# A gated mix of a long convolution and a two-row expert: forward transforms by four token residues and 256 frequencies, with VectorE additions behind them and a new table of order

## The chip, the cores and the metric

The kernel runs on one core of one Trainium2 chip. A core has five engines with a queue each: TensorE (PE in the profile, its weight loads PEld), VectorE (DVE), ScalarE (ACT), GpSimd (POOL) and SyncE (SP). Each engine takes its instructions in the order in which they stand in its queue; semaphores tie the queues together. TensorE writes to psum, eight banks of 512 float32 per partition; everything else lies in one large buffer of on-chip memory that the program calls RB. The metric is device time in microseconds, the median of the runs.

## The reference, cut to what matters

```python
# u: 2048 tokens x 512 channels (bf16), A, B, C: 512 x 128, complex
dt = exp(log_dt)[:, None]
P = exp((dt * A)[:, :, None] * arange(2048))           # all powers
K = einsum("dn,dnl,dn->dl", C, P, dt * B).real         # 512 kernels, 2048 long
y = irfft(rfft(pad(u)) * rfft(pad(K)))[:2048]          # a causal convolution per channel
a = y + u * Dskip
r = u @ w_r                                            # the two rows with the largest r
x2 = u[top2(r)]                                        # go through a gated MLP
b = u, with sigmoid(r) * ((silu(x2 @ w_gate) * (x2 @ w_up)) @ w_down) added to these two rows
g = sigmoid((u * gate_w).sum(-1))
out = g * a + (1 - g) * b
```

## The kernel before

The convolution is done with transforms that are matmuls with constant cosine and sine matrices. The 2048 tokens are two blocks m of 1024. Of each block the matmuls of the forward transform make 512 frequencies (four groups of 128, in two pairs kp), real and imaginary (the planes pl), for 512 channels. The tokens of a block stand as u(q, r): q is the half, r the residue of the token number modulo 4, with 128 tokens on the partitions.

`forward` (L716) makes one psum tile of two banks, 128 frequencies x 512 channels in each. For a plane and a pair kp, `product(par)` runs 8 matmuls of 128x512: two frequency groups, and four token groups (two halves, the two residues r = par and par + 2). First the odd residues (par 1) are accumulated, and `store` writes them scaled by -2 (fwo); then the even ones (par 0) are added into the same banks, and the sum is written (fwe). POOL then issues two accumulating transfers inside on-chip memory (ACC, L421, called vb), which add the second to the first: even tokens plus odd tokens, and even minus odd. That gives 1024 frequencies from 512. The frequency that lies 1024 higher needs no matmul of its own. The stores can be done by ScalarE (L403) or VectorE (L409, L733). Per block this is 64 matmuls (L723), eight stores of 1024 columns and four transfers of 256 KB.

The kernels K are built from powers: ScalarE makes exponentials of the decays (ep, eq; `AF`, L412) and sines of phases (sin), TensorE the phases (pa, L605, L606, L625, L627) in fixed point, VectorE multiplies them (`coarse`: pi, pr; `fine`: px, py, ps; all by `TT`, L387). `lags` multiplies coarse and fine powers on TensorE (kmm, L900, L901), evacuates them (kae), selects (sel, L914; kcx, kce), and `spectrum` turns them into spectra KH (ks, L941; khe). `products` multiplies spectra (prod, yr, yi, pq, b0, b2, b13 on VectorE; ac on TensorE with the stores ace), and `inverse` transforms back (iv, L1082 to L1087) with the stores ive (L1098, L1102) and the output transfers.

Beside it runs the routing: a transposed load of u (xt, L424, issued by SyncE), log (L660) with its copies rs, rf, the two largest rows (gm, gm2, L678 to L681), the gather gu, and the MLP (ff, dn, with transfers of its three weight matrices). Other names in the prediction: al and bs are the first VectorE instructions, on the loaded A; arg (L586) are phase arguments; dth is exp(log_dt) on ScalarE and dtn its cast on VectorE (L406); np (L400) are eight products of B and C with dtn; nw transposes their sums on TensorE, kw stores them; k0e, k0c store a row for lag 0; ns negates sines (L632).

What sets the order: the program adds its operations in one list; each names what it reads and writes and the engines that may do it. PLAN holds for every place in the order the number of an operation and which of its engines does it; BANKS holds a psum bank for each tile. `replay` (L111) walks PLAN and `emit_plan` (L135) puts each operation into its engine's queue with the waits that its data need. So a change of PLAN moves work between engines and in every queue. On chip memory is cut into regions by hand: F holds the forward matrix, later the constants of the spectra (kn); U holds u, then the second block's transform and small constants; V the transforms.

The lines where the accumulating transfer and the forward matmuls stand:

```python
def ACC(name, vs, rd, wr, kb):
    return P.add(name, [(POOL, 1.5 * len(vs), lambda h: [h.dma_start(out=o(), in_=a_(), accum_op=ALU.add) for o, a_ in vs])], ...)
...
for i, (q, r) in enumerate((q, r) for q in range(2) for r in (par, par + 2)):
    x = h.matmul(P32(t, k2, ...), FM(0, 128, pl * 4096 + (par * 4 + i) * 512 + (2 * kp + k2) * 128, (1, 128)), U(..., ((m * 2 + q) * 4 + r) * 512, (1, 512)), ...)
```

## Time and profile before

| | us |
|---|---|
| three runs | 152.25, 152.31, 152.98 |
| median | 152.31 |
| the profiled execution | 152.89 |
| its span, first to last instruction | 151.0 |

| engine | busy, us | instructions |
|---|---|---|
| TensorE | 139.5 | 1603 |
| VectorE | 135.5 | 186 |
| ScalarE | 116.5 | 173 |
| POOL | 27.6 | 34 |

The span is some 2 us shorter than the execution that it was taken from; the rest lies around the first and the last instruction. "Busy" counts an engine that executes; an idle engine is charged to whatever released it. A row of a view with "x60 | 71.6, 1221 | 0.7" says: 60 instructions, 71.6 us busy in all, 1221 ns for one, 0.7 us of idle time before them. A row of the view in order of time begins with its start and its length. Instructions of one engine can overlap at their ends, so the busy time of a group is a little less than count times mean.

### The profile page before, as it was taken

The numbers are of one execution on the slowest core, as the hardware profiler recorded it, in microseconds if no ns is written. First come the engines' busy times: TensorE is split into PE (matmuls) and PEld (weight loads), VectorE is DVE, ScalarE is ACT, GpSimd is POOL, SyncE is SP. The second block draws the span as 40 slices with busy tenths as digits, with TensorE's granted clock in tenths as the row PEclk, the third lists the DMA queues.
The fourth block names the chain that finished last, engine by engine and source line by source line (L and its number), as shares of the span: only waits on it lengthen the run. The fifth ranks groups of instructions, "written<-read, shape, count | busy, mean of one in ns | idle before, by whom it ended". The sixth has DMA issues, their size and how long they took to land.

```text
span 151.0 us, 3726 instructions
## 1 busy us (share of the span) xinstructions
PE 139.5 (92%) x1603; PEld 100.5 (67%) x1603; DVE 135.5 (90%) x186; ACT 116.5 (77%) x173; POOL 27.6 (18%) x34
## 2 busy tenths in 40 slices
PE   3799999999999999999875999999999999999990
PEld 2257776444664665898845889856878767776870
DVE  0699899999999999999999999999999999994941
ACT  4697998999999897667972778877994773379830
POOL 5000001300010199679206200220000000000000
PEclk9999999999999999999999999999999999999999
DMA  3899899980893096799971500018930009400176
GB/s 77 238 270 286 293 411 413 407 329 13 289 358 121 0 538 295 197 288 195 190 114 13 96 0 4 4 23 270 276 148 4 0 0 253 166 4 0 35 208 174
DMA packets 23107, 26.43 MB, mean 175 GB/s; under 512 B 9486, under 2 KB 20244, under 8 KB 22420
## 3 DMA queue, kind: packets, MB, share of 16 engines
q1 hardware_dynamic: 20644, 23.98, 49.3%
q0 software_dynamic: 2304, 2.10, 9.1%
q8 instruction: 12, 0.20, 0.5%
q10 hardware_dynamic: 144, 0.13, 0.4%
q14 instruction: 3, 0.02, 0.0%
HBM read 19.78 MB, written 4.20 MB: 159 GB/s over the span
## 4 chain that ended last, share of the span: by engine, by line
PE 55%; DVE 36%; issue 4%; DMA 1%; ACT 1%; SPq 0%; DVEq 0%
DVE RB L387 33%; PE psm L723 18%; PE psm L1087 7%; PE psm L1004 4%; PE psm L625 4%; PE psm L491 4%; PE psm L627 2%; PE psm L605 2%; PE psm L786 2%; PE psm L1082 2%; PE psm L1006 2%; PE psm L1008 2%; PE psm L660 1%; PE psm L531 1%; PE psm L606 1%
## 5 line engine op out<-in xcount | busy, mean ns | idle before, releaser
L387 DVE TENSOR_TENSOR RB<-RB 128x2048 bf16<-128x2048 bf16 (+6 forms) x113 | 106.8, 994 | 3.4 <-ACT RB L403 2.5
L403 ACT ACTIVATE RB<-psm 128x1024 bf16<-128x1024 f32 (+6 forms) x52 | 46.9, 944 | 13.0 <-PE psm L1008 7.3
L723 PE MATMUL psm<-RB 128*128 128x512 bf16 x128 | 29.1, 379 | 0.0
L412 ACT ACTIVATE RB<-RB 128x512 bf16<-128x512 f32 (+6 forms) x48 | 27.1, 646 | 1.7 <-DVE RB L387 1.6
L412 ACT ACTIVATE RB<-psm 128x1024 bf16<-128x1024 int16 (+2 forms) x23 | 21.6, 976 | 6.1 <-PE psm L627 4.4
L723 PEld LDWEIGHTS psm<-RB 128*128 128x128 bf16 x128 | 12.3, 98 | 13.2
L1087 PE MATMUL psm<-RB 128*128 128x256 bf16 x128 | 18.9, 273 | 0.0
L900 PE MATMUL psm<-RB 128*128 128x80 bf16 x256 | 17.5, 198 | 0.0
L901 PE MATMUL psm<-RB 128*128 128x64 bf16 x256 | 17.5, 191 | 0.0
L900 PEld LDWEIGHTS psm<-RB 128*128 128x128 bf16 x256 | 17.0, 96 | 0.6 <-DVE RB L387 0.2
L901 PEld LDWEIGHTS psm<-RB 128*128 128x128 bf16 x256 | 16.9, 97 | 0.1
L941 PE MATMUL psm<-RB 128*128 128x256 bf16 x128 | 14.3, 273 | 2.0 <-ACT RB L403 2.0
L941 PEld LDWEIGHTS psm<-RB 128*128 128x128 bf16 x128 | 12.4, 98 | 4.1 <-ACT RB L403 2.7
L1087 PEld LDWEIGHTS psm<-RB 128*128 128x128 bf16 x128 | 12.5, 98 | 1.6
L1098 ACT ACTIVATE RB<-psm,RB 128x256 bf16<-128x256 f32 x25 | 9.9, 478 | 3.1 <-PE psm L1087 3.1
L421 POOL DMA_DIRECT2D RB<-RB x8 | 9.9, 2188 | 2.4 <-ACT RB L403 2.4
L1004 PE MATMUL psm<-RB 128*128 128x512 bf16 x32 | 10.2, 379 | 0.2 <-DVE RB L387 0.2
L625 PE MATMUL psm<-RB 128*128 128x256 f16 x64 | 9.0, 273 | 0.5 <-ACT RB L412 0.5
L397 POOL CAST RB<-RB 128x16 bf16<-128x16 f32 (+4 forms) x6 | 6.9, 1165 | 12.9 <-DVE RB L670 12.8
L1082 PE MATMUL psm<-RB 128*128 128x256 bf16 x32 | 8.7, 273 | 0.0
L409 DVE CAST RB<-psm 128x1024 bf16<-128x1024 f32 (+3 forms) x7 | 7.2, 1025 | 0.9 <-PE psm L555 0.7
L625 PEld LDWEIGHTS psm<-RB 128*128 128x128 f16 x64 | 6.1, 98 | 2.2 <-ACT RB L412 0.8
(77 smaller groups left out, 161.3 us busy)
## 6 DMA issues: line engine op xcount, KB each, us to landing
RB<-c_fwd SPq DMA_DIRECT2D x2, 1024.0 KB, 8.0
RB<-in_A_u_dram SPq DMA_DIRECT2D x2, 1024.0 KB, 6.8
RB<-c_near SPq DMA_DIRECT2D x2, 1024.0 KB, 5.4
RB<-RB POOLq DMA_DIRECT2D x8, 256.0 KB, 9.0
RB<-u_routed SPq DMA_DIRECT2D x2, 1024.0 KB, 5.4
RB<-in_B_w_gate_dram SPq DMA_DIRECT2D x1, 1792.0 KB, 14.1
RB<-in_B_w_up_dram SPq DMA_DIRECT2D x1, 1792.0 KB, 14.3
RB<-in_B_w_down_dram SPq DMA_DIRECT2D x1, 1792.0 KB, 8.6
```

The source lines that it names most:

```text
L387: return P.add(name, [(eng, c_dve(n, mode) if eng == DVE else 1.6, lambda h: h.tensor_tensor(out=o(), in0=a_(), in1=b_(), op=op))], rd, wr ...
L403: return lambda h: h.activation(out=o(), in_=a_(), func=ACTF.Copy, scale=scale() if callable(scale) else scale)
L412: return P.add(name, [(ACT, cost or c_act(n), lambda h: h.activation(out=o(), in_=a_(), func=func, scale=scale))], rd, wr, table=table, **kw)
L421: return P.add(name, [(POOL, 1.5 * len(vs), lambda h: [h.dma_start(out=o(), in_=a_(), accum_op=ALU.add) for o, a_ in vs])], rd, wr, dma=(4 ...
L625: r = h.matmul(o, DGM(0, 128, d * 128, (1, 128)), HL(0, 128, z * 512 + hf * CW, (1, CW)), start=(u == 0 and z == 0 and i % 2 == 0), stop=F ...
L723: x = h.matmul(P32(t, k2, 0, 128, 0, (1, 512)), FM(0, 128, pl * 4096 + (par * 4 + i) * 512 + (2 * kp + k2) * 128, (1, 128)), U(0, 128, ((m ...
L900: h.matmul(P32(t, q // 6, 0, 128, (q % 6) * 80, (1, 80)), tp, TQv(0, 128, c * 10240 + ri * NT2 * 256 + r * 4, (256, NT2), (1, 4)), start=( ...
L901: x = h.matmul(P32(t, q // 6, 0, 128, (q % 6) * 80 + 16, (1, 64)), tp, ARENA(0, 128, eY[c][ri][0] + r * 4, (eY[c][ri][1] - eY[c][ri][0], 2 ...
L941: x = h.matmul(o, KN(0, 128, g * 2048 + col, (1, 128)), KC[c](0, 128, g * 256, (1, 256)), start=(g == 0), stop=(g == NG - 1))
L1004: r = h.matmul(P32(t, kt, 0, 128, 0, (1, 512)), CI(0, 128, 0, (1, 128)), f(k, 0, 512), start=(k == 0 and hc == 1), stop=False, skip_group_ ...
L1082: h.matmul(o, RD(0, 128, (tb + 8) % 16 * 128, (1, 128)), UE[q](0, 128, r * 256, (1, 256)) if early else U2(0, 128, tb * D + c * CW, (1, 25 ...
L1087: x = h.matmul(o, G(0, 128, (pl * 2 + kt // 2) * 1024 + (r * 2 + q) * 128, (1, 128)), PQ(0, 128, r * 1024 + kt * 256 + pl * 256 if quarter ...
```

## The change

The forward transform now makes one psum tile for each pair of residues. It computes only 256 frequencies (every other group of 128), but keeps the four residues apart: the two banks of a tile hold two residues instead of two frequency groups, and each takes 2 matmuls (the two halves) instead of 4. With z = 1 the tile holds residues 2 and 3, with z = 0 residues 0 and 1 added to them; the stores are scaled as before, and vb adds in the same way as before, now even and odd residues apart. A second step follows for each block: vs adds and subtracts the odd sums to the even sums, vt does the same with the quarter-turned differences (real and imaginary planes exchanged). That gives the same 1024 frequencies. Per block this is 32 matmuls instead of 64, the same eight stores and four transfers, and four VectorE instructions (`TT`) of 2048 elements per partition.

The forward matrix is half as large (two loads of 512 KB instead of 1024) and its region F lies elsewhere; its freed half holds some of the transform (fodd), which the first load of kn overwrites later. PLAN and BANKS are new throughout.

```diff
-PLAN = [(0, 0), (4, 0), (21, 0), (3, 0), (1, 0), (41, 0), (22, 0), (42, 0), (174, 0), ...
+PLAN = [(4, 0), (5, 0), (6, 0), (0, 0), (21, 0), (3, 0), (1, 0), (41, 0), (22, 0), (42, 0), (234, 0), ...
...
-    a = [np.outer(BLK + token(0, q, r), theta()) for par in range(2) for q in range(2) for r in (par, par + 2)]
+    th = theta().reshape(4, 128)[::2].reshape(256)
+    a = [np.outer(BLK + token(0, q, r), th) for r in range(4) for q in range(2)]
...
         def forward(m, pl, kp, behind):
             t = P.pst(2, "fw", (0, 2))
-            def product(par):
+            def product(z):
                 def fw(h):
                     x = None
                     for k2 in range(2):
-                        for i, (q, r) in enumerate((q, r) for q in range(2) for r in (par, par + 2)):
-                            x = h.matmul(P32(t, k2, 0, 128, 0, (1, 512)), FM(0, 128, pl * 4096 + (par * 4 + i) * 512 + (2 * kp + k2) * 128, (1, 128)), U(0, 128, ((m * 2 + q) * 4 + r) * 512, (1, 512)),
-                                         start=(par == 1 and i == 0), stop=(par == 0 and i == 3), skip_group_check=True)
+                        r = 2 * z + k2
+                        for q in range(2):
+                            x = h.matmul(P32(t, k2, 0, 128, 0, (1, 512)), FM(0, 128, pl * 2048 + ((r * 2 + q) * 2 + kp) * 128, (1, 128)), U(0, 128, ((m * 2 + q) * 4 + r) * 512, (1, 512)),
+                                         start=(z == 1 and q == 0), stop=(z == 0 and q == 1), skip_group_check=True)
                     return x
...
         def transform(m, behind=()):
...
-                ACC("vb", [(v(1, z), v(0, z)) for z in range(2)], [bV[m][0][pl], bVO[m][pl]], [bV[m][1][pl]], 512)
+                ACC("vb", [(vat(m, 1, 1024 - 512 * pl, (1, 512)), vat(m, 0, 1024 + 512 * pl, (1, 512))), (fodd(m, 512 * pl, (1, 512)), vat(m, 1, 1536 * pl, (1, 512)))], bFE(m, 0, pl) + bFE(m, 1, pl) + bOD(m, pl) + [bFO[m][pl]], bFE(m, 1, pl) + [bFO[m][pl]], 512)
+            e0, e1, od = [b[0] + b[1] for b in ([bFE(m, 0, pl) for pl in range(2)], [bFE(m, 1, pl) for pl in range(2)], [bOD(m, pl) for pl in range(2)])]
+            even, odd = vat(m, 0, 1024, (512, 2), (1, 512)), vat(m, 1, 0, (1536, 2), (1, 512))
+            TT("vs", vat(m, 0, 0, (512, 2), (1, 512)), even, odd, ALU.add, e0 + od, bV[m][0][0], 2048)
+            TT("vs", even, even, odd, ALU.subtract, e0 + od, e0, 2048)
+            quad, turn = vat(m, 1, 1024, (-512, 2), (1, 512)), fodd(m, 512, (-512, 2), (1, 512))
+            TT("vt", odd, quad, turn, ALU.add, e1 + bFO[m], od, 2048)
+            TT("vt", quad, quad, turn, ALU.subtract, e1 + bFO[m], e1, 2048)
```

The new table also gives some work of VectorE to ScalarE: one fwo store, one fwe store, three ns, k0e, a kcx, a kae, a k0c and two ive stores; one ace store goes the other way. ScalarE loads its function tables four times instead of five.

How the queues changed, at the places that the prediction speaks of. All names in these rows are RB and psm, so the lines tell the operations; the new file's lines lie 2 higher than those of before up to the transform, and up to 14 higher behind it.

SyncE, the first transfers. Before (in_A_B and in_A_C are the four inputs of np, in_A_u with DMA_TRANSPOSE is xt):

```order
L478 DMA RB<-in_A_log_dt_dram 1x512
L479 DMA RB<-c_id 128x128
L481 DMA RB<-in_A_A_im_dram 128x512
L498 DMA RB<-c_diag 128x896
L517 DMA RB<-in_A_Dskip_dram 1x512
L524 DMA RB<-in_A_log_dt_dram 128x4
L481 DMA RB<-in_A_B_re_dram 128x512
L481 DMA RB<-in_A_C_re_dram 128x512
L498 DMA RB<-c_diag 128x512
L481 DMA RB<-in_A_B_im_dram 128x512
L481 DMA RB<-in_A_C_im_dram 128x512
L424 DMA_TRANSPOSE RB<-in_A_u_dram 128x4x2048
```

and now:

```order
L480 DMA RB<-in_A_log_dt_dram 1x512
L481 DMA RB<-c_id 128x128
L483 DMA RB<-in_A_A_im_dram 128x512
L500 DMA RB<-c_diag 128x896
L526 DMA RB<-in_A_log_dt_dram 128x4
L426 DMA_TRANSPOSE RB<-in_A_u_dram 128x4x2048
L483 DMA RB<-in_A_C_re_dram 128x512
L483 DMA RB<-in_A_B_im_dram 128x512
L483 DMA RB<-in_A_B_re_dram 128x512
L483 DMA RB<-in_A_C_im_dram 128x512
L500 DMA RB<-c_diag 128x512
L520 DMA RB<-c_f 128x160
```

The transposing load moved ahead of the four inputs of np and of one part of c_diag; Dskip moved behind.

VectorE and ScalarE, the first instructions. VectorE now (L588 is arg, the CAST of 128x4 at L408 is dtn, the COPY from psm is log, L402 of 128x256 is np):

```order
L588 TENSOR_SCALAR RB<-RB 128x512
L389 TENSOR_TENSOR RB<-RB 128x512
L588 TENSOR_SCALAR RB<-RB 128x512 x7
L408 CAST RB<-RB 128x4
L588 TENSOR_SCALAR RB<-RB 128x512
L408 COPY RB<-psm 128x32
L588 TENSOR_SCALAR RB<-RB 128x512
L408 CAST RB<-RB 128x16 x2
L680 TENSOR_REDUCE RB<-RB 128x1
L402 SCALAR_TENSOR_TENSOR RB<-RB 128x256 x6
```

ScalarE now, between its first activation and its second table load (128x128x4 are ep, 128x2x256 and 128x512 are eq, 128x4 is dth):

```order
L414 ACTIVATE RB<-RB 128x128x4 x3
L414 ACTIVATE RB<-RB 128x2x256
L414 ACTIVATE RB<-RB 128x128x4
L414 ACTIVATE RB<-RB 128x2x256 x3
L414 ACTIVATE RB<-RB 128x128x4 x2
L414 ACTIVATE RB<-RB 128x2x256 x3
L414 ACTIVATE RB<-RB 128x128x4
L414 ACTIVATE RB<-RB 128x2x256
L414 ACTIVATE RB<-RB 128x128x4 x2
L414 ACTIVATE RB<-RB 128x4
L414 ACTIVATE RB<-RB 128x128x4
L414 ACTIVATE RB<-RB 128x512
```

Before, seven large activations stood ahead of dth, and VectorE had four arg ahead of dtn, the eight np mixed with further arg behind it, and log only after kw and the first weights. Now 17 stand ahead of dth, eight arg ahead of dtn, and log stands ahead of all np.

VectorE in the middle, the second half of the coarse powers with the new instructions. Now (128x2x64x16 are pi and pr, L634 is ns, 128x2x1024 and 128x2x2x512 are vs and vt):

```order
L389 TENSOR_TENSOR RB<-RB 128x2x64x16
L389 TENSOR_TENSOR RB<-RB 128x2x1024
L389 TENSOR_TENSOR RB<-RB 128x2x64x16
L389 TENSOR_TENSOR RB<-RB 128x2x1024
L634 TENSOR_SCALAR RB<-RB 128x1024
L389 TENSOR_TENSOR RB<-RB 128x2x64x16 x2
L389 TENSOR_TENSOR RB<-RB 128x2x2x512
L389 TENSOR_TENSOR RB<-RB 128x2x64x16
L389 TENSOR_TENSOR RB<-RB 128x2x1024
L389 TENSOR_TENSOR RB<-RB 128x2x64x16 x2
L389 TENSOR_TENSOR RB<-RB 128x2x2x512
L389 TENSOR_TENSOR RB<-RB 128x2x64x16
```

The two first rows of 128x2x1024 are vs of block 0; vt and the ones of block 1 follow between the coarse factors, all before the second half of the fine powers. Before, pi and pr stood there with ns, the px and py of the fine powers and one kae store between them.

46 lines of the change are left out of this document (25 added, 21 removed), and 67 rows, old and new, of the table PLAN.

## The prediction

> **What bounds the kernel now.** I read the page first (busy time of each engine, then the chain that ended last), then the busy time by stretch, then VectorE's waits, then the rows by shape.
>
> ```profile
> PE 139.5 (92%) x1603; PEld 100.5 (67%) x1603; DVE 135.5 (90%) x186; ACT 116.5 (77%) x173; POOL 27.6 (18%) x34
> PE 55%; DVE 36%; issue 4%; DMA 1%; ACT 1%; SPq 0%; DVEq 0%
> DVE RB L387 33%; PE psm L723 18%; PE psm L1087 7%; PE psm L1004 4%; PE psm L625 4%; PE psm L491 4%; PE psm L627 2%; PE psm L605 2%; PE psm L786 2%; PE psm L1082 2%; PE psm L1006 2%; PE psm L1008 2%; PE psm L660 1%; PE psm L531 1%; PE psm L606 1%
> ```
>
> The chain seems to convict TensorE: 55% of the span, and the forward matmuls of L723 alone 18%. These are what the change halves. But a chain shows one engine that was busy, not that the others had time to spare. The stretches show that. I cut at 4.25 us (VectorE's first instruction), at 62.7 (where the chain passes from TensorE to VectorE) and at 134.8 (the end of the last two products).
>
> ```profile
> 4.25:62.70 58.45, 57.42 (x517) 34.79 (x517) 55.66 (x95) 54.05 (x77) 12.64 (x17) 1.00 0.83 277
> 62.70:134.80 72.10, 68.22 (x984) 55.47 (x981) 71.49 (x77) 51.54 (x78) 12.82 (x12) 1.00 0.47 115
> 134.80:151.00 16.20, 12.13 (x103) 9.38 (x100) 8.33 (x15) 9.07 (x18) 0.00 (x0) 1.00 0.33 97
> ...
> DVE RB L387 <- PE psm L531: 4.3, 1, 4.3
> DVE RB L387 <- ACT RB L403: 2.5, 3, 2.0
> DVE RB L1102 <- PE psm L1087: 2.0, 3, 1.1
> DVE RB L409 <- PE psm L555: 0.7, 1, 0.7
> DVE RB L400 <- PE psm L531: 0.7, 1, 0.7
> DVE RB L400 <- issue: 0.2, 1, 0.2
> DVE RB L733 <- PE psm L723: 0.2, 1, 0.2
> ```
>
> Behind the length of a stretch stand the busy times of TensorE, its weight loads, VectorE, ScalarE and POOL. VectorE is busy 55.66 of 58.45 us, then 71.49 of 72.10. From its first instruction to 134.8 it does nothing for 3.4 us in all. So in the first stretch both engines are full, and TensorE's relief is worth to VectorE only what VectorE waits for TensorE there: 0.7 (L400), 0.7 (L409), 0.2 (L733). The wait of 4.3 is the start, behind the first loads; those of 2.5 and 2.0 lie in the last 16.2 us. VectorE's own work between 4.25 and 134.8 therefore sets the end, with some 16 us of tail behind it.
>
> **The work that VectorE gains and loses.**
>
> ```profile
> L387 DVE TENSOR_TENSOR RB<-RB 128x2048 bf16<-128x2048 bf16 x60 | 71.6, 1221 | 0.7
> L733 DVE TENSOR_SCALAR RB<-psm 128x1024 bf16<-128x1024 f32 x4 | 4.8, 1212 | 0.2 <-PE psm L723 0.2
> L409 DVE CAST RB<-psm 128x1024 bf16<-128x1024 f32 x3 | 3.7, 1222 | 0.8 <-PE psm L555 0.7
> L632 DVE TENSOR_SCALAR RB<-RB 128x1024 bf16<-128x1024 bf16 x7 | 2.9, 411 | 0.0
> L409 DVE CAST RB<-psm 32x512 bf16<-32x512 f32 x2 | 1.4, 696 | 0.1
> L409 DVE CAST RB<-psm 128x960 bf16<-128x960 f32 x1 | 1.2, 1158 | 0.0
> L919 DVE COPY RB<-RB 32x256 bf16<-32x256 bf16 x1 | 0.2, 223 | 0.0
> L403 ACT ACTIVATE RB<-psm 128x1024 bf16<-128x1024 f32 x36 | 35.3, 1021 | 9.3 <-PE psm L1008 7.3 <-PE psm L941 1.7 <-PE psm L946 0.3
> L723 PE MATMUL psm<-RB 128*128 128x512 bf16 x128 | 29.1, 379 | 0.0
> ```
>
> Added: eight tensor-tensor instructions of 128x2048 bf16 (vs twice and vt twice, for two blocks). Shape and type are those of the first row, and all inner runs are 512 long. 71.6 us over 60 is 1.19 each, so 9.5 us. Where such an instruction does not wait for the one before it, they follow each other closer, and in dependent pairs a little wider; I give the sum 0.5 us either way.
>
> Taken off VectorE and put on ScalarE by the new table: one fwo store (1.21), one fwe store (1.22; the row's third is kw and stays), three negations ns (3 x 0.41 = 1.23), k0e and kcx (2 x 0.70), a kae (1.16) and a k0c (0.22). That is 6.4. Net before the last products: +3.1 us. ScalarE does the big ones in about 1.0 us (its row), at 54.05 of 58.45 busy in the first stretch and 51.54 of 72.10 in the second; the moves come late in the first stretch or in the second, where there is room, and it saves a table load.
>
> TensorE loses 64 of 128 matmuls at 29.1/128 = 0.23 us, 14.5 us. All of it lies beside VectorE's work, so I cost it at nothing. If VectorE were not the cover, it would be worth 14.5.
>
> **The front, where the order is new.** Here a step is moved past queues. SyncE now issues the transposing load of u ahead of the four loads of B and C; ScalarE runs 17 exponentials before dth instead of seven large activations; VectorE has dtn and log ahead of the products np.
>
> ```profile
> 8.63 1.43 DVE L586 TENSOR_SCALAR RB<-RB 128x512 int32<-128x512 f32 x4
> 9.97 0.17 DVE L406 CAST RB<-RB 128x4 f32<-128x4 bf16 x1
> ...
> 4.97 5.41 ACT L412 ACTIVATE RB<-RB 128x512 bf16<-128x512 f32 x11 [1.63 <-DVE RB L387]
> 27.41 4.37 ACT L412 ACTIVATE RB<-RB 128x512 bf16<-128x512 f32 x9
> ...
> 2.49 0.29 SPq L517 DMA_DIRECT2D RB<-in_A_Dskip_dram  x1
> 3.22 0.43 SPq L481 DMA_DIRECT2D RB<-in_A_B_re_dram  x1
> 5.61 8.14 SPq L424 DMA_TRANSPOSE RB<-in_A_u_dram  x1
> RB<-in_A_u_dram SPq DMA_TRANSPOSE x1, 10.1
> RB<-in_A_C_im_dram SPq DMA_DIRECT2D x1, 128.0 KB, 3.2
> ...
> 18.11 2.26 PE L660 MATMUL psm<-RB 128*128 128x2 bf16 x64
> ```
>
> First dtn. ScalarE's exponentials start behind al at 4.97. Eleven there, one of them the tiny dth, take 5.41: 0.52 for a large one (the second row, eight large and one tiny in 4.37, says the same). Seventeen end at 4.97 + 8.8 = 13.8, dth at 14.0. VectorE comes to dtn after eight arg instructions (1.34 us for four, from 8.63 to 9.97): 8.63 + 2.7 = 11.3. It waits 2.7 us.
>
> Then log. The transposing load was issued at 5.61; the loads of B and C, one of c_diag and that of Dskip (0.34 from its start to the next) no longer stand ahead, so it starts at 3.22 - 0.34 = 2.9, lands 10.1 later at 13.0, and TensorE's 64 small matmuls take 2.26: log can be read at 15.3. VectorE is there at 14.0 + 0.17 + 0.42 = 14.6: another 0.7. Queued behind are arg, rs, gm and np, thus all of VectorE. np does not wait again: its four loads are issued from 2.9 + 8.1 = 11.0 on, about 0.48 apart (five in 3.22 to 5.61), the last near 12.5, and land 3.2 later at 15.7; np comes at about 16.4. The two waits are 3.4 us. Two old ones go: kw's 0.7, since its weights are now ready behind other work, and the 0.2 called issue. Net +2.5.
>
> **The accumulating transfers.** vs overwrites what vb reads, and vt needs its sums, so VectorE now waits in order for POOL's transfers; before, only the products far behind did.
>
> ```profile
> L421 POOL DMA_DIRECT2D RB<-RB x8: 1209/1929/3651, 59.7 to 69.0; - x8
> DMA to landing us min/median/max: 6.9/9.0/11.1
> ```
>
> For the first block I estimate the last store some 3 us behind VectorE's last fwo (seven large ScalarE instructions and a table load follow an sge that waits for ffe, against 5 us of VectorE from ffe to fwo); the second issue and the landing add 1.2 + 9.0 (at most 11.1): 13 to 15. From that fwo VectorE has eleven large and eight small instructions to do before the vs that waits, 11 x 1.2 + 2.4 = 15.6 us: hidden, narrowly. For the second block the last fwe follows a coarse sine that waits for a pr of VectorE, 1.9 us behind it; with 1.2 + 9.0 that is 12.1, and VectorE does ten large ones and a negation (12.4 us) between. Even, so I take 0; with the slowest landing it costs 1.8, which goes into the upper bound. The queued victims would be vs, vt and the second coarse factors, then kmm and the spectra.
>
> **The tail.**
>
> ```profile
> 138.83 0.38 PE L1087 MATMUL psm<-RB 128*128 128x256 bf16 x2
> 146.11 0.82 PE L1087 MATMUL psm<-RB 128*128 128x256 bf16 x6
> L1102 DVE TENSOR_TENSOR RB<-psm,RB 128x512 bf16<-128x512 f32 x3 | 2.1, 692 | 2.0 <-PE psm L1087 2.0
> L1102 DVE TENSOR_TENSOR RB<-psm,RB 128x256 bf16<-128x256 f32 x1 | 0.4, 421 | 0.0
> ```
>
> An ace store comes to VectorE (1.22) and two ive go from it (0.69 + 0.42). VectorE may lose 1 us of its wait for ScalarE there, but from 138.8 to the end of the row at 146.11 TensorE runs the inverse matmuls nearly without a gap, and their number and order behind the last products are as before. 16.2 us stay: 0, at best -0.5.
>
> **Sum.** 151.0 + 3.1 + 2.5 = 156.6 us of span. The profiled execution took 152.89, 1.9 more than its span, and lies 0.6 above the median 152.31. So 156.6 + 1.9 - 0.6 = 157.9; I say 157.8.
>
> **Rivals.**
>
> A, the sum above: 157.8; of its own 155.8 to 159.6.
>
> B, the work comes but not the front wait: the exponentials or the load are earlier than I work out, or the planner's order leaves VectorE something to do. 151.0 + 3.1 - 0.9 = 153.2 of span, 154.5. For it: the load now has less traffic ahead. Against it: dth and log bind independently, and each alone costs over 2 us.
>
> C, TensorE at half rate at log, so that the routing and everything behind is later still.
>
> ```profile
> 6.39 3.17 PE L491 MATMUL psm<-RB 128*128 128x512 bf16 x7 [0.78 <-DVE RB L400]
> 15.07 1.02 PE L491 MATMUL psm<-RB 128*128 128x512 bf16 x4
> ```
>
> Seven warm-up matmuls of one shape take 3.17 us early (0.45 each), four take 1.02 later (0.22 to 0.25), while the granted clock reads 1.00 throughout. Of the 16 warm-up matmuls in front, two now stand before the first use, two more before the forward transforms; the rest are moved to the middle. TensorE has nothing between about 5.6 and 9 us. If the 64 matmuls of log pay double, 2.3 us: 160.1. If they are bound by issue, nothing. The Trainium skill, "TensorE: Matmul & The Clock Gate", Part 1, says that the array runs at half its clock until some 3.4 us of sustained work, and falls back after an idle window as long. By that rule the pair of rows above is the rise, and C is likelier than not to cost part of its price; the granted clock in this trace does not show it.
>
> D, not slower: the chain is right, TensorE's 14.5 us come off the first 62.7, and the new additions fill holes. 151.0 - 14.5 + 9.5 = 146.0, or 147.3 by the median. For it: TensorE is busy 57.42 of 58.45. It decides only if VectorE's instructions, or their order, leave it 14.5 us to give; its idle time before 62.7 is 2.8. That is what speaks against it.
>
> **Chances.** A 0.60, B 0.18, C 0.14, D 0.05, and 0.03 for the sums of small gains that end near no change. Half a per cent is about what a measurement of this kernel can tell from none. Faster by more than that: D with a little, 0.06; within: 0.03; slower: 0.91. The range takes A and C whole and B's centre: 154.2 to 160.8 (C with a part of the 1.8 of the transfers).
>
> **What would show it.** VectorE's busy time near 138.6 and TensorE's near 125. A first VectorE wait of 2 to 3 us at the small cast dtn, released by ScalarE, and a shorter one at the copy of log, released by TensorE. The forward matmuls gone from the chain, VectorE's share above half. vs and vt at 1.2 us, with less than 2 us of waits for transfers. The last products ending near 140. It is wrong if VectorE is found idle for less than 3 us up to there (B), if its work did not grow by about 3, or if the tail shrank by more than 1.

## The result, and the profile after

| | before | after |
|---|---|---|
| runs, us | 152.25, 152.3, 152.31, 152.98 | 166.37, 166.71, 167.26, 167.92 |
| median | 152.31 | 166.99 |
| the profiled execution, and its span | 152.89, 151.0 | 166.71, 164.9 |
| granted clock over the span | 1.0 | 0.935 |

The ratio is 1.096, with an interval of 1.090 to 1.102. The prediction said 157.8, with a range to 160.8: the direction was right, the size was not. Of some variants below, single runs were granted a lower clock and took up to 5 us longer; the times given for these variants, like the ratios, leave such runs out.

First the page: busy time, the granted clock, and the chain.

```profile
PE 133.6 (81%) x1532; PEld 96.5 (59%) x1539; DVE 136.8 (83%) x184; ACT 122.7 (74%) x183; POOL 30.9 (19%) x34
PEclk9999569965699999999999699999999999999998
DVE 39%; PE 27%; DMA 16%; ACT 13%; issue 2%; POOL 0%; SPq 0%; DVEq 0%
DVE RB L389 31%; DMA RB<-RB 10%; PE psm L1101 7%; ACT RB L405 7%; ACT RB L414 5%; DMA RB<-in_A_u_dram,RB 5%; PE psm L1018 4%; DVE RB L402 3%; PE psm L607 2%; PE psm L1022 2%; PE psm L1020 2%; DVE RB L411 2%; PE psm L608 2%; PE psm L1096 2%; PE psm L662 1%
```

The forward matmuls (L729) have left the head of the chain, as the change means them to. But VectorE's share is 39%, not above half, and two kinds of transfer stand in a chain that had 1% of them: those inside on-chip memory (10%) and the gather (5%). VectorE's busy time hardly rose (135.5 to 136.8). So the 14 us are not work. The busy time by stretch, cut at VectorE's first instruction, around its longest idle time, and at the end of the last two products:

```profile
4.27:75.03 70.76, 52.86 (x585) 34.62 (x588) 61.82 (x100) 64.29 (x90) 25.96 (x26) 0.88 0.84 236
75.03:81.89 6.86, 6.83 (x143) 5.47 (x139) 0.00 (x0) 6.43 (x8) 0.00 (x0) 1.00 0.61 146
81.89:148.60 66.71, 58.95 (x703) 45.75 (x706) 66.47 (x70) 40.96 (x66) 2.82 (x1) 0.97 0.26 85
148.60:164.90 16.30, 12.17 (x103) 9.48 (x101) 8.53 (x15) 9.19 (x20) 0.00 (x0) 0.97 0.34 98
```

The third number with a count in brackets is VectorE's. It is busy 61.82 of 70.76 us, then for 6.86 us not at all, then 66.47 of 66.71. The tail is 16.30 us (16.20 before). Up to the last products VectorE works 61.82 + 66.47 = 128.29 us; before, the two stretches gave 55.66 + 71.49 = 127.15. Idle it is for 16.0 us, against 3.4. The whole difference of the spans, 13.9, is therefore +1.1 of work, +12.6 of waits and +0.1 of tail. VectorE's waits (total, times, longest) name them:

```profile
DVE RB L389 <- DMA RB<-RB: 6.9, 1, 6.9
DVE RB L408 <- ACT RB L414: 3.4, 1, 3.4
DVE RB L411 <- PE psm L729: 1.7, 1, 1.7
DVE RB L408 <- PE psm L662: 1.4, 1, 1.4
DVE RB L408 <- PE psm L707: 1.4, 1, 1.4
DVE RB L411 <- PE psm L557: 0.5, 1, 0.5
```

The first is the second vs of block 1, waiting for its accumulating transfers: 6.9 us, of which the prediction had 0, at most 1.8. L408 behind ScalarE is dtn, and L408 behind L662 is log: 3.4 and 1.4 (predicted 2.7 and 0.7). L408 behind L707 is xs, which waits for the gathered rows, and L411 behind L729 is the fwe store queued behind it on TensorE: 3.0 us together (1.37 and 1.66), and in no term of the sum. Behind 82 us there is no wait of this size until the tail.

Now the two unforeseen ones in order of time (start, length, engine). First the transfers of block 1 on POOL's queue, SyncE's issues, and the vs that ends the wait:

```profile
61.76 2.41 POOL L423 DMA_DIRECT2D RB<-RB  x2 [2.18 <-ACT RB L405]
63.90 0.34 SPq L1138 DMA_DIRECT2D RB<-c_near  x1
64.28 2.02 SPq L1140 DMA_DIRECT2D RB<-in_A_u_dram  x4
65.43 2.40 POOL L423 DMA_DIRECT2D RB<-RB  x2 [0.87 <-ACT RB L405]
66.34 0.86 SPq L832 DMA_DIRECT2D u_routed<-in_A_u_dram  x1
67.24 0.60 SPq L1139 DMA_DIRECT2D RB<-c_far  x1
81.89 15.09 DVE L389 TENSOR_TENSOR RB<-RB 128x2048 bf16<-128x2048 bf16 x13 [6.86 <-DMA RB<-RB]
```

The last two transfers are issued from 65.43 on, and vs can run at 81.89, 16.5 us later. Among them SyncE issues, in a row, the first load of kn (L1138, 1 MB), the four small loads u8 (L1140), the copy of u into u_routed (L832, called uc, 2 MB) and kf (L1139, 512 KB). Before, the first load of kn and uc went out ahead of all accumulating transfers, whose first was issued at 59.73:

```profile
52.11 0.34 SPq L1124 DMA_DIRECT2D RB<-c_near  x1
52.49 0.66 SPq L818 DMA_DIRECT2D u_routed<-in_A_u_dram  x1
```

Then the gather: POOL's issue of it, VectorE's instructions beside it, and TensorE behind it:

```profile
29.45 3.98 POOL L702 DMA_INDIRECT RB<-in_A_u_dram,RB  x1 [6.88 <-DVE RB L402]
29.06 3.48 DVE L389 TENSOR_TENSOR RB<-RB 128x2048 bf16<-128x2048 bf16 x3
32.46 1.21 DVE L741 TENSOR_SCALAR RB<-psm 128x1024 bf16<-128x1024 f32 x1
38.21 0.26 PE L707 MATMUL psm<-RB 2*128 2x2 bf16 x4 [2.92 <-DMA RB<-in_A_u_dram,RB]
38.40 1.89 PE L729 MATMUL psm<-RB 128*128 128x512 bf16 x4
```

POOL needs 3.98 us to issue the gather, where it needed 1.02 before:

```profile
29.24 1.02 POOL L700 DMA_INDIRECT RB<-in_A_u_dram,RB  x1 [0.21 <-issue]
```

VectorE runs three products of 2048 elements (zm) in that time. The gathered rows reach TensorE at 38.21 (gat), which has waited 2.9 us for them, and the four forward matmuls behind it take 1.89 us, 0.47 each, twice the 0.23 that a matmul of this shape took on average before.

### The profile page after: what moved, and what is told of

It is laid out like the page before. It is cut to its first block, busy times and chain, and to the rows that moved or that the text cites. A ratio compares the mean times of both kernels' runs of the same rounds, so it can differ in the third digit from the quotient of the medians.

```text
span 164.9 us, 3598 instructions
## 1 busy us (share of the span) xinstructions
PE 133.6 (81%) x1532; PEld 96.5 (59%) x1539; DVE 136.8 (83%) x184; ACT 122.7 (74%) x183; POOL 30.9 (19%) x34
## 3 DMA queue, kind: packets, MB, share of 16 engines
q1 hardware_dynamic: 20644, 22.93, 43.8%
## 4 chain that ended last, share of the span: by engine, by line
DVE 39%; PE 27%; DMA 16%; ACT 13%; issue 2%; POOL 0%; SPq 0%; DVEq 0%
DVE RB L389 31%; DMA RB<-RB 10%; PE psm L1101 7%; ACT RB L405 7%; ACT RB L414 5%; DMA RB<-in_A_u_dram,RB 5%; PE psm L1018 4%; DVE RB L402 3%; PE psm L607 2%; PE psm L1022 2%; PE psm L1020 2%; DVE RB L411 2%; PE psm L608 2%; PE psm L1096 2%; PE psm L662 1%
## 5 line engine op out<-in xcount | busy, mean ns | idle before, releaser
L389 DVE TENSOR_TENSOR RB<-RB 128x2048 bf16<-128x2048 bf16 (+7 forms) x121 | 114.4, 1003 | 7.5 <-DMA RB<-RB 6.9
L405 ACT ACTIVATE RB<-psm 128x1024 bf16<-128x1024 f32 (+6 forms) x56 | 50.9, 948 | 26.7 <-PE psm L955 13.3
L414 ACT ACTIVATE RB<-psm 128x1024 bf16<-128x1024 int16 (+2 forms) x23 | 22.4, 993 | 3.6 <-PE psm L608 1.7
L955 PE MATMUL psm<-RB 128*128 128x256 bf16 x128 | 15.6, 286 | 6.2 <-issue 5.8
L729 PE MATMUL psm<-RB 128*128 128x512 bf16 x61 | 16.7, 406 | 4.6 <-DVE RB L741 3.1
L1101 PE MATMUL psm<-RB 128*128 128x256 bf16 x128 | 19.0, 273 | 0.0
L955 PEld LDWEIGHTS psm<-RB 128*128 128x128 bf16 x128 | 13.0, 103 | 9.2 <-issue 6.3
L914 PEld LDWEIGHTS psm<-RB 128*128 128x128 bf16 x256 | 17.0, 97 | 0.9 <-ACT RB L405 0.6
L915 PEld LDWEIGHTS psm<-RB 128*128 128x128 bf16 x256 | 16.9, 97 | 0.1
L1101 PEld LDWEIGHTS psm<-RB 128*128 128x128 bf16 x128 | 12.5, 98 | 1.5
L729 PEld LDWEIGHTS psm<-RB 128*128 128x128 bf16 x64 | 5.9, 101 | 11.0 <-DVE RB L741 3.6
L1112 ACT ACTIVATE RB<-psm,RB 128x256 bf16<-128x256 f32 x28 | 11.1, 485 | 0.8 <-PE psm L1101 0.8
L833 POOL DMA_INDIRECT u_routed<-RB x1 | 2.8, 2822 | 39.5 <-DVE RB L389 39.5
L627 PE MATMUL psm<-RB 128*128 128x256 f16 x64 | 10.1, 291 | 0.1
L1018 PE MATMUL psm<-RB 128*128 128x512 bf16 x29 | 9.5, 380 | 0.7 <-ACT RB L405 0.6
L629 PE MATMUL psm<-RB 128*128 128x256 f16 x40 | 7.7, 289 | 2.4 <-ACT RB L414 2.4
L399 POOL CAST RB<-RB 128x16 bf16<-128x16 f32 (+4 forms) x6 | 6.4, 1082 | 16.7 <-DVE RB L408 16.7
L1096 PE MATMUL psm<-RB 128*128 128x256 bf16 x32 | 8.7, 273 | 0.0
```

The source lines that it names most:

```text
L389: return P.add(name, [(eng, c_dve(n, mode) if eng == DVE else 1.6, lambda h: h.tensor_tensor(out=o(), in0=a_(), in1=b_(), op=op))], rd, wr ...
L405: return lambda h: h.activation(out=o(), in_=a_(), func=ACTF.Copy, scale=scale() if callable(scale) else scale)
L414: return P.add(name, [(ACT, cost or c_act(n), lambda h: h.activation(out=o(), in_=a_(), func=func, scale=scale))], rd, wr, table=table, **kw)
L627: r = h.matmul(o, DGM(0, 128, d * 128, (1, 128)), HL(0, 128, z * 512 + hf * CW, (1, CW)), start=(u == 0 and z == 0 and i % 2 == 0), stop=F ...
L729: x = h.matmul(P32(t, k2, 0, 128, 0, (1, 512)), FM(0, 128, pl * 2048 + ((r * 2 + q) * 2 + kp) * 128, (1, 128)), U(0, 128, ((m * 2 + q) * 4 ...
L914: h.matmul(P32(t, q // 6, 0, 128, (q % 6) * 80, (1, 80)), tp, TQv(0, 128, c * 10240 + ri * NT2 * 256 + r * 4, (256, NT2), (1, 4)), start=( ...
```

## The experiments

Most edits are to the order: pairs in PLAN are moved, and with them places in the engines' queues. Pairs that only slide along are not shown.

### What is late at vs: the copy

```diff
-... (163, 0), (288, 0), (290, 0), (169, 0), (339, 0), ...
+... (163, 0), (288, 0), (290, 0), (339, 0), ...
-... (304, 0), (333, 0), (9, 0), ...
+... (304, 0), (333, 0), (169, 0), (9, 0), ...
```

169 is uc, 333 the load of c_inv.

> One edit: SyncE issues the copy of u into u_routed (2 MB, off chip to off chip) behind the second load of kn and the load of c_inv instead of at 66.3 us, between the accumulating transfers of block 1 and the vs that waits for them. Theory 1 (the transfers share the queues): in the changed kernel the queues had kn, u8, uc, kf and vb to move between 61.8 and 81.8; at the 317 GB/s that the hardware queue shows over its run (22.93 MB in 43.8% of 164.9 us) 2 MB are 6.6 us. Without them vb lands at about 75.2, the wait of 6.9 us at vs shrinks below 1, and the time falls by 5.5 to 7 from 167.0, to 160 to 161.5. Rival (the accumulating transfers are slow by themselves, or what waits is their completion): the wait stays above 5 and the time within 1 us. A smaller fall with a new wait for khe behind the load of kn would say that the copy costs in its new place.

161.73 us (161.12 to 162.33), ratio 1.060 (1.055 to 1.064). POOL's second pair of issues, the vs that waits, and uc in its new place:

```profile
66.55 2.40 POOL L423 DMA_DIRECT2D RB<-RB  x2 [0.92 <-ACT RB L405]
77.60 15.10 DVE L389 TENSOR_TENSOR RB<-RB 128x2048 bf16<-128x2048 bf16 x13 [1.46 <-DMA RB<-RB]
84.26 0.66 SPq L832 DMA_DIRECT2D u_routed<-in_A_u_dram  x1
```

One transfer that nothing near it needs cost 5.3 us of the 14.7. vs now runs 11.1 us behind that issue (77.60 - 66.55), 5.4 sooner; the estimate from the queue's rate was 6.6. The rival, transfers slow by themselves, falls. That 1.5 us of wait were left fits the other loads there, kn and kf.

### Why the gather is late: VectorE or the queues

Two kernels, of one idea each: gather_psum puts a store that reads psum behind the first of the three zm (so the row of products breaks off), gather_wu sends the 1.8 MB of w_up behind the gather.

```diff
# gather_psum: 104, 106 = forward matmuls and their fwo store, 189, 190, 186 = zm
-... (189, 0), (190, 0), (186, 0), (104, 0), (106, 1), ...
+... (189, 0), (104, 0), (106, 1), (190, 0), (186, 0), ...
# gather_wu: 151 = w_gate, 192 = second block of u, 154 = w_up
-... (186, 0), (104, 0), ... (151, 0), ... (154, 0), ... (192, 0), ...
+... (186, 0), (151, 0), (192, 0), (154, 0), (104, 0), ...
```

> One edit: VectorE does the fwo store that reads psum behind the first of the three 128x2048 products zm instead of behind the third; these products ran from 29.06 to 32.5 while POOL issued the gather (29.45, 3.98 us long instead of 1.02 before the change). Theory 2 (POOL cannot write the gather's descriptors while VectorE runs a row of bf16 products): the issue ends about 1.5 to 2 us sooner, at 31 to 32, the gather lands as much sooner, and the waits at xs and fwe (1.4 and 1.7) shrink together by 1.5 to 2; time 165 to 165.5 if nothing takes it back later. Rival (the gather is late since the 1.8 MB of w_up are under way): issue length and waits unchanged, time within 0.5 of 167.0.

> One edit: SyncE issues the load of w_up (1.8 MB) behind that of the second block of u, so at about 33 us instead of 27.5, behind the gather's issue. Rival of theory 2 (the gather waits for its share of the queues): its issue takes about 1 us, it lands at about 35, the waits at xs and fwe (3.0 together) go, time 164 to 164.5. Theory 2 (VectorE's products hold POOL up): the issue stays near 4 us, the landing gains 1 us at most. Either way w_up lands at about 42 and the second ff, at 44 to 45, should not wait; if it does, that is a cost of the edit.

The issue and VectorE beside it (start, length) in gather_psum:

```profile
29.16 1.71 POOL L702 DMA_INDIRECT RB<-in_A_u_dram,RB  x1 [6.73 <-DVE RB L402]
28.77 1.21 DVE L389 TENSOR_TENSOR RB<-RB 128x2048 bf16<-128x2048 bf16 x1
29.91 1.21 DVE L741 TENSOR_SCALAR RB<-psm 128x1024 bf16<-128x1024 f32 x1
```

and gather_wu:

```profile
28.87 3.98 POOL L702 DMA_INDIRECT RB<-in_A_u_dram,RB  x1 [6.30 <-DVE RB L402]
28.48 3.48 DVE L389 TENSOR_TENSOR RB<-RB 128x2048 bf16<-128x2048 bf16 x3
```

The length of the issue doesn't come from the queues: with w_up out of the way the issue still lasts 3.98 us. In all three kernels it ends 0.89 us behind the row of products that it met: in the changed kernel at 33.43, the row at 32.54; here at 30.87 and 29.98; in gather_wu at 32.85 and 31.96. Theory 2 holds for the gather, not for every transfer that POOL issues: the accumulating ones are not held. Their second pair took 2.40 us from 65.43 on, 1.20 each, in the middle of nine products in a row (10.46 us from 64.57 on). The Trainium skill, "SBUF — State Buffer", section "SBUF: two separate sides", says that an instruction of VectorE with two inputs in on-chip memory and one of GpSimd that reads this memory lock each other out of a port that they share, for the length of the one that came first. The products have two such inputs, and the gather reads its row numbers in RB: these rows agree, with the lock held over three products in a row.

In gather_psum the waits at xs and fwe fell from 3.0 to 0.6 us, and 0.9 came back at an ns. The time: 165.17 and 165.84 us, so 1.2 to 1.8 less. The wait at vs stayed at 7.0. gather_wu took 165.07 and 166.70 us, which can't be told from gather_psum; its waits can, 0.85 and 1.66 at xs and fwe. So the cause is shown by the issue and the waits, not by these times; what the waits are worth, the next kernel shows.

### Both together

```diff
# the edits of copy_late and gather_psum, and kf (289) behind the second load of kn (287)
-... (214, 0), (289, 0), (287, 0), ...
+... (214, 0), (287, 0), (289, 0), ...
```

> Three edits of the order together: the copy into u_routed behind the load of c_inv (as in copy_late), the load of kf (512 KB) from beside it to behind the second load of kn, and the fwo store behind the first zm (as in gather_psum). Theory 1 with theory 2: copy_late left a wait of 1.5 us at vs, 512 KB are 1.6 us at 317 GB/s, so that wait goes; gather_psum's 2.5 us at xs and fwe, which the queues took back there, now reach the end. From 161.7: 161.7 - 1.5 - 2.5 = 157.7, so 157 to 158.7. If theory 1 is wrong about what is left at vs, 159 to 160.2. If kf in its new place makes khe late, a wait at the first products shows it.

158.09 us (157.84 to 158.99), ratio 1.035 (1.030 to 1.040): inside what was expected. VectorE from its first instruction to the last products, and the tail:

```profile
4.12:140.92 136.80, 117.90 (x1424) 85.85 (x1432) 128.41 (x170) 111.84 (x162) 27.51 (x27) 0.94 0.60 171
140.92:157.20 16.28, 12.17 (x103) 9.45 (x101) 8.52 (x15) 9.19 (x20) 0.00 (x0) 1.00 0.35 98
```

It works 128.41 us there, as much as in the changed kernel (128.29), and is idle for 8.4 instead of 16.0. VectorE itself waits for no transfer any more. The time is 3.6 us below copy_late: 1.5 for the wait that was left at vs there, and some 2 for the gather. So three moved operations give back 8.9 of the 14.7 us, with every matmul and every addition of the change in place.

### The front

Five kernels tried to bring the front's waits back to what they were. front_order, on the changed kernel, undoes three moves:

```diff
# SyncE, 36 = the transposing load; ScalarE, 38 = dth; VectorE, 39 = dtn, 46 to 53 = np
-... (221, 0), (173, 0), (175, 0), ... (37, 0), (38, 0), ... (39, 0), (150, 0), (36, 0), ... (29, 0), (28, 0), (27, 0), (30, 0), (52, 0), ...
+... (221, 0), (173, 0), (2, 0), (23, 0), (37, 0), (29, 0), (27, 0), (26, 0), (28, 0), (30, 0), (38, 0), ... (148, 0), (39, 0), (52, 0), ... (36, 0), ... (64, 0), ...
```

> The order of the front put back on three queues: the four loads for np and one of c_diag ahead of the transposing load, dth behind six exponentials instead of 17, and dtn behind four arg, with np and the other arg between it and log. The prediction's theory (dth and the transposing load bind one after the other): the wait of 3.4 at dtn goes; the load lands at 5.3 + 10.5 = 15.8, log can be read at 18.1, and VectorE, with 6.3 us of work behind dtn at 9.7, comes there at 16.1: a wait of 2.0 instead of 1.4, and some tenths more between the steps of gm, whose fillers are gone. Net 2 to 2.8 us less at log. If it reaches the end, 164.2 to 165; if the late landing of the accumulating transfers takes it (their time is set by the queues, not by VectorE), the wait at vs grows by as much and the time stays near 167.

168.41 us (167.64 to 169.08): no gain. The waits moved and kept their sum:

```profile
DVE RB L408 <- PE psm L662: 2.9, 1, 2.9
DVE RB L683 <- PE psm L682: 2.3, 2, 1.6
```

dtn's 3.4 are gone, log's 1.4 became 2.9, and 2.3 appear between the steps of gm, where np had been the filler. 5.5 us before the edit, 5.4 with it, and the gather issued at 29.48 instead of 29.45. all_three, on both_waits, adds other work ahead of log:

```diff
# as front_order, and TensorE's phases of the weights (125, 127) and nw (56, 57), VectorE's kw (58), wx, wx, wp (129 to 131) ahead of log (63, 64);
# ten exponentials of the decays (234, 233, 217, 221, 246, 227, 240, 232, 223, 236) behind the sines (147)
```

> The edits of both_waits, and the front rearranged so that VectorE has other work while log is awaited: the four loads for np ahead of the transposing load, dth behind two exponentials, the ten large exponentials of the decays behind the sines, TensorE's phases of the weights and nw ahead of log, and np, ns2, kw and three products of the weights ahead of log on VectorE. In front_order the sum of the waits up to the gather stayed at 5.5 us (3.4 at dtn became 2.9 at log and 2.3 between the steps of gm). Theory 3 (what the front costs is not one wait but the lack of other work for VectorE until log): with kw and the weights' products ahead of log these waits fall to 2 to 3 us and the time 2.5 to 3.5 below both_waits: 154.5 to 155.5. Rival (TensorE's phases and the sines come too late for that work, since TensorE runs at half rate until 13.6): the waits only move to kw and wx, and the time is within 0.8 of both_waits.

158.91 us (158.23 to 159.86), against 158.09: as the rival said. kw waited 2.65 us, the steps of gm 2.7 in all.

> The edits of all_three, and six of the warm-up matmuls moved from the middle to the front, behind the transposes of the loaded A, where TensorE has nothing to do from about 5 to 8.3 us. In all_three the phases behind that gap run at half pitch (0.21 us for 256 columns where later 0.11 are seen) until 13.4, ScalarE waits 1.3 us for them, and kw comes 2.65 us late. Rival C's mechanism (TensorE at half rate in the front): with TensorE kept at work the phases run at full pitch, the second sine starts 1.3 us sooner, kw's wait falls from 2.65 to about 1.3, and the time from 158.9 to 157.4 to 157.9. If the rate doesn't follow from the idle time ahead, the phases keep 0.21 us and start 2.6 us later behind the warm-ups: time 159 to 161.

158.94 us (158.39 to 159.13), not to be told from all_three. The mechanism was there, the gain was not. TensorE in the front: the warm-ups, the first two matmuls of the phases, and two of them 3.6 us later (256 columns each)

```profile
4.98 2.85 PE L493 MATMUL psm<-RB 128*128 128x512 bf16 x6
8.63 0.61 PE L607 MATMUL psm<-RB 128*128 128x256 f16 x2 [0.80 <-DVE RB L389]
12.24 0.38 PE L607 MATMUL psm<-RB 128*128 128x256 f16 x2
```

The phases ran at half pitch only from 8.63 to 11.80 (0.21 us for 256 columns, then 0.11), where in all_three they did until 13.4, and kw waited 1.8 us instead of 2.65. hybrid takes the order of before on every engine up to place 130 in its PLAN (without the first coarse phases and k0e, for want of psum banks) and that of both_waits behind it. hybrid2 exchanges zm there.

```diff
# VectorE's order from the mask of gm (83) to the fine powers: 84, 88 = gm, 86, 90 = gm2, 99 = idx, 115, 106 = fwo, 186 to 188, 190 = zm
-hybrid:  83, 187, 84, 86, 87, 88, 186, 90, 99, 115, 106, 191, 133, 188, 190
+hybrid2: 83, 186, 84, 86, 87, 88, 188, 90, 99, 115, 106, 191, 133, 190, 187
```

> The edits of both_waits (the copy and kf later, a psum store behind the gather's issue), and everything up to the gather in the order of before on every engine: the loads, the exponentials, 15 warm-up matmuls, the phases of the weights and log behind them, VectorE's kw and the weights' products ahead of log, and behind log the chain of gm with a zm and a weights' product between its steps. In before and in half_only this front held VectorE up for 1.65 and 1.3 us from its first instruction to the gather; both_waits and all_three show 6.2 and 6.9. Theory 3 (the front's order, not one of its waits, is what costs): the waits fall to 1.3 to 2 and the time by 4.2 to 4.9 from 158.1: 153.2 to 153.9, within 1% of before. Rival (the middle of the changed order needs the exponentials that ScalarE did early in its own front, or the second transform comes no sooner): new waits between 30 and 60 us take it back, 156.5 or more.

> hybrid with two products exchanged: there the zm that stands between the steps of gm read the root that ScalarE makes last (the exponential behind the second table load, ready at 26.9), and VectorE waited 3.17 us for it; now the zm stand there whose roots and sines are ready before 23, and that one comes behind the gather's issue. Theory 3 as amended (the front costs what VectorE cannot fill): that wait goes and the others of the front (2.9 together) stay, so 3 us less than hybrid, which had 159.6: 156.3 to 157, the nearest to before of all orders with the second step. If the wait only moves to the next product, 158.5 or more.

hybrid: 159.63 us (159.02 to 160.63). hybrid2: 158.9 to 159.2 us, where 156.3 to 157 was expected. hybrid lost 3.17 us at one zm that reads the last exponential; with that gone, hybrid2 waits 1.1 and 1.3 us at an ffe and at a ns behind the gather. Every order of the front that was tried leaves VectorE 5.8 to 9.2 us of waits between its start and 50 us, where before has 1.8. So theory 3 isn't shown by them. Which part of the old order it is that no rearrangement gave back is left open.

### What TensorE's relief is worth

half_only is the order of before, with half of the forward matmuls and no second step; old_order adds vs and vt. In both, the load of kn that goes out second (by number the program's first, as the expectation calls it) must wait: in half_only for vb, whose result lies in its way, in old_order for vt. Two more transfers moved in half_only: the copy uc to 39.26 (52.49 before), and the load of kn that goes out first to 58.50 (52.11 before).

```diff
# half_only, in place of vs, vs, vt, vt
+            TT("vs", vat(m, 0, 0, (512, 2), (1, 1)), vat(m, 0, 1024, (512, 2), (1, 1)), vat(m, 0, 1024, (512, 2), (1, 1)), ALU.add, e0, bV[m][0][0], 4)
# the PLAN of before, renumbered; the second load of kn behind the last vb
# old_order: the same with the change's vs and vt, and kn behind the last vt
```

> The order of before with half the forward matmuls and without the second step (vs and vt are left out but for one addition of 4 elements for each block, so the output isn't the reference's); the first load of kn waits for the accumulating transfers, whose result lies where it goes. It measures what TensorE's relief is worth by itself. The prediction's theory (VectorE covers all of it): 152.3 to 153.5, the latter if the late kn makes khe late by 1 us. Rival D (TensorE's 14.5 us come off): 138 to 141. Something between would say that the relief is worth a part.

> The change's arithmetic in the order of before: half the matmuls, vs and vt between the fine powers of the second half, none of the moves from VectorE to ScalarE, the first load of kn behind vt. The prediction's theory (each addition costs VectorE its length): 152.3 + 9.5 = 161.8, and up to 3 us more where khe waits for kn: 161.5 to 165. If it is below 159, the additions cost less than their length; if it is 165 or more, most of the loss lies in the dependence of kn on vt, not in the work. Compared with the changed kernel at 167.0 it says what the new order as a whole is worth: by the waits seen there, -6.4 of work and +12.6 of waits, so old_order should be the faster by 2 to 5 us.

half_only 156.46 us (156.09 to 157.31), 4.1 slower than before: rival D is out, and the forecast of no change was too good. old_order 169.53 (168.64 to 170.11): 13.1 more, of which 9.3 are work (VectorE busy 144.7, against 135.4) and 3.8 a longer wait for khe (5.37 against 1.55). It is also slower than the changed kernel, not faster as expected: the new order as a whole is worth 2.5 us. The question of half_only's 4.1 was settled by making the load late in the kernel before. A first try, before_kn_late, moved it in the order only; nothing made SyncE wait, the load went out at 60.55, and the kernel took 152.79, which tells nothing.

> The kernel before the change with one edit: SyncE issues the second load of kn (1 MB) behind the last accumulating transfers, as half_only has to, at about 80 us instead of 60.4. In half_only VectorE waited 0.7 for a kae's psum, 1.6 and 0.3 for khe and 1.6 at kcx, 4.1 in all, which is its whole loss. Theory 4 (the late load makes the spectra late, and those four waits follow from it): 155.5 to 156.7, with the waits for khe and kcx. Rival (TensorE at a lower rate, granted clock 0.944 in half_only against 1.00): 152.3 to 153, since this kernel has all its matmuls.

```diff
# before_kn_dep, behind the loads of kn
+        P.ops[279].deps.update(o for o in P.ops if o.name == "vb")
```

> The kernel before the change with one edit: the second load of kn waits for all the accumulating transfers, as in half_only (in before_kn_late it was only moved behind them in SyncE's order, nothing made it wait, and it was issued at 60.6 as ever). It goes out at about 80 us. Theory 4 (half_only's loss of 4.1 us comes from this late load): waits of VectorE for khe and kcx as in half_only, 155.5 to 156.7. Rival (it comes from TensorE's gaps and lower rate): 152.3 to 153.

156.80 us (156.15 to 157.44). Its waits are those of half_only, nearly to the tenth; first half_only, then before_kn_dep (start and length of the instruction, its wait in brackets):

```profile
89.76 2.29 DVE L388 TENSOR_TENSOR RB<-RB 128x4096 bf16<-128x4096 bf16 x1 [1.55 <-ACT RB L404]
105.04 0.96 DVE L410 CAST RB<-psm 128x768 bf16<-128x768 f32 x1 [1.56 <-PE psm L924]
```

```profile
89.72 2.29 DVE L387 TENSOR_TENSOR RB<-RB 128x4096 bf16<-128x4096 bf16 x1 [1.70 <-ACT RB L403]
105.01 0.96 DVE L409 CAST RB<-psm 128x768 bf16<-128x768 f32 x1 [1.55 <-PE psm L914]
```

(L410 and L409 are kce here, not kcx.) So the late load by itself costs as much as half_only lost. Between these two kernels, halving the matmuls gains 0.3 us, which can't be told from the prediction's 0. half_twice does half_only's matmuls twice:

```diff
-                        for q in range(2):
+                        for q in (0, 0, 1, 1):
```

> half_only with each forward matmul done twice, so that TensorE has as much to do as before the change and no more gaps than there; the late load of kn stays, the second step is left out as in half_only, and the output isn't the reference's. Theory 4: 155.8 to 157, as half_only at 156.5. Rival (gaps and rate): the waits go, and 152.3 to 154.

159.39 us (158.53 to 160.44): more than expected by either side, so the rival is out, and something comes on top. By this pair the halving is worth 2.9 us, not 0.3. The wait for khe is 4.16 there. The first load of kn, which waits for the last forward matmul, goes out at 60.42 instead of half_only's 58.50, thus later among the accumulating transfers; the second, which waits for these, at 79.02 instead of 77.48. It looks as if 2.9 us of TensorE's time came back through the loads, but that was not taken apart: the relief is worth between 0.3 and 2.9 us, far from the 14.5 of rival D, and which of the two is open.

### Whether VectorE's work sets the end before

```diff
# before_moves: ns (340, 347), kae (295), kcx (305) and the k0c of the second half (389) to ScalarE
-... (340, 0), ... (295, 1), ... (347, 0), ... (305, 1), ... (389, 0), ...
+... (340, 1), ... (295, 0), ... (347, 1), ... (305, 0), ... (389, 1), ...
# before_stores: the same without 340 and 347
```

> The kernel before the change with five operations of VectorE on ScalarE behind 62 us, as the change has them (two ns, one kae, kcx and the k0c of the first half), and one back (the k0c of the second half): VectorE loses 0.82 + 1.16 + 0.70, 2.7 us; nothing of the arithmetic is changed. The prediction's theory of the bound (VectorE is busy 71.49 of 72.10 us there, and the end follows it; ScalarE has 20 us to spare): 152.4 - 2.7 = 149.7, between 149.5 and 150.5. If ScalarE's later spectra or a later ns take it back, a wait at the first products or at pi, and 152 or more. It is the change's good part alone, and faster than both kernels if the bound is where the prediction put it.

> The kernel before the change with one kae, kcx and the k0c of the first half on ScalarE (and the k0c of the second half back on VectorE), without the negations of before_moves, for which VectorE waited 4.66 us. VectorE loses 1.16 + 0.70, 1.9 us. The prediction's theory of the bound: 152.4 - 1.9 = 150.5, between 150 and 151, faster than both kernels. If ScalarE's later spectra take it back, waits for khe or kcx of as much and 152 or more.

before_moves 155.56 us (154.08 to 155.89; ratio 1.017, 1.013 to 1.021), before_stores 153.90 (153.74 to 155.18; ratio 1.010, 1.006 to 1.014): both slower than before, though VectorE works 2.8 and 1.9 us less. (The k0c moved is that of the second half, and none went back, other than the expectations say.) Of before_moves and before_stores, the new waits:

```profile
72.16 9.67 DVE L387 TENSOR_TENSOR RB<-RB 128x2048 bf16<-128x2048 bf16 x8 [4.66 <-ACT RB L403]
```

```profile
73.94 6.01 DVE L387 TENSOR_TENSOR RB<-RB 128x2048 bf16<-128x2048 bf16 x5 [0.85 <-ACT RB L403]
102.68 0.96 DVE L409 CAST RB<-psm 128x768 bf16<-128x768 f32 x1 [1.27 <-PE psm L914]
```

With ns on ScalarE, pi waits 4.66 us for it. Even without that, two products of the coarse powers wait 0.39 and 0.85, and kce 1.27. VectorE had no slack, but ScalarE and TensorE stand close behind it in the loop phases, sine, ns, pi. No version beats the kernel before.

### TensorE's rate behind the gather

```diff
# warm_gat, on both_waits: seven warm-ups (9 to 15) ahead of gat (101)
+... (108, 0), (9, 0), (10, 0), (11, 0), (12, 0), (13, 0), (14, 0), (15, 0), (101, 0), ...
```

> both_waits with seven warm-up matmuls moved from the middle to TensorE's queue ahead of gat, where TensorE has waited 3.0 us for the gathered rows; behind that gap its matmuls ran at half pitch from 36.2 to about 46 us (0.47 us for 512 columns, 0.21 for 256). Rival C's mechanism (idle time halves the rate, for a while): the warm-ups take 1.5 us of the gap, the forward matmuls and phases behind gat run at 0.24 and 0.11, VectorE's waits there (0.41 at fwe, 1.10 at ns) go, and the time falls by 1 to 1.5 from 158.1, to 156.6 to 157.1. If the rate doesn't follow from the gap, the half pitch stays and the time is 157.7 to 158.5.

157.1, 158.3 and 158.8 us; both_waits had 157.8 to 159.0. The four matmuls behind gat, in both_waits and then here:

```profile
36.23 1.89 PE L729 MATMUL psm<-RB 128*128 128x512 bf16 x4
```

```profile
36.47 1.04 PE L729 MATMUL psm<-RB 128*128 128x512 bf16 x4
```

They run at full pitch, and VectorE's waits at fwe and ns (0.41 and 1.10) are gone, but the gain is within what the runs differ.

## Why the prediction was wrong

**The bound** was right as far as it went: in old_order the 9.3 us that VectorE works more than in half_only appear in the time in full. (That its work and waits add up to the span shows nothing by itself; they would for any engine.) It didn't hold in the other direction, as before_moves and before_stores show: in both, less work on VectorE brought new waits and no gain.

**The work term**, +3.1, came out at +1.1. The row of these products grew by 7.7 us, not by 9.5:

```profile
L389 DVE TENSOR_TENSOR RB<-RB 128x2048 bf16<-128x2048 bf16 x68 | 79.3, 1214 | 7.1 <-DMA RB<-RB 6.9
```

That is 79.3 - 71.6 of the same row before. The additions were priced rightly: in old_order the same row has 80.8 us, 9.2 more. In the new order such products follow each other closer: nine took 10.46 us from 64.57 on, 1.16 each, where before eight took 9.76 from 69.57 on, 1.22 each. The prediction named this effect and gave it 0.5 us; it is worth 1.5 to 1.8. What left VectorE was 6.6 by difference (7.7 - 1.1), for 6.4. This was an error of size, in the favourable direction.

**The front**, +2.5, was right in mechanism (dtn behind ScalarE, log behind TensorE, np without a wait) and 2.1 too small in its waits. dth was done at 14.06 (forecast 14.0), but VectorE was there at 10.66 instead of 11.3, because a wait of 0.7 us for TensorE at its start (L400), which the sum had kept, was gone; log could be read at 15.94 (forecast 15.3), and kw kept 0.5 of the wait that was to go. In exchange some 1.9 us of other waits and gaps that the sum had carried over from before were gone, that wait of 0.7 among them.

**The accumulating transfers** are the step that failed. For block 0 "hidden, narrowly" was right. For block 1 the prediction wrote "even, so I take 0; with the slowest landing it costs 1.8". Its landing time, 6.9 to 11.1, was that of before, taken as a property of the transfer. In the changed kernel the same view reads:

```profile
DMA to landing us min/median/max: 3.9/6.5/15.7
```

The time depends on what the queues carry at that moment. The new order had put a copy of 2 MB, which in before was issued 7 us ahead of the accumulating transfers, and 1.5 MB of loads between their issue and the wait. copy_late and both_waits show the price: 6.9 us. SyncE's queue was read at the front, and not there.

**The gather** is the second failure, 3.0 us of waits: the prediction followed np and log, and not what the new order puts beside the gather's issue on VectorE. gather_psum shows the cause, both_waits that some 2 us of it reach the end.

With the two taken away the kernel takes 158.1, near the 157.8 of rival A. That is in part luck: VectorE works 128.41 us there up to the last products, where the sum had 130.25 (127.15 + 3.1), and is idle for 8.4, where the sum had 5.9 (3.4 + 2.5). An error of 1.8 one way and one of 2.5 the other nearly cancel.

**TensorE's relief at nothing** was right within 3 us: half_only and before_kn_dep differ by 0.3, half_only and half_twice by 2.9, which is open. Rival D with its 147.3 is refuted. But its busy time fell by 5.9 us, not by 14.5:

```profile
L729 PE MATMUL psm<-RB 128*128 128x512 bf16 x61 | 16.7, 406 | 4.6 <-DVE RB L741 3.1 <-DVE RB L683 0.8 <-ACT RB L405 0.6
```

The forward matmuls (61 of the 64 are on record) went from 29.1 to 16.7 us, 0.27 us of busy time each instead of 0.23, and the phases in front and in the middle took longer by 5. TensorE now has gaps, and part of what follows them runs at half pitch.

**The tail**, 16.20 forecast and 16.30 measured, was right. **Rival C** was wrong where it was put: the 64 matmuls of log take 2.26 us as before. Its mechanism struck elsewhere, at the phases and behind the gather. **Rival B** (no front wait) is refuted: the waits there are larger than forecast.
